# One weight piece converted per tile from tile 1 on, its clamp on GpSimdE, and other assumed VectorE times

## The chip, the cores and the metric

The kernel runs on one core of a Trainium2 chip. The time is device microseconds of one execution; runs of one kernel agree within a fraction of a per cent, and the time of a kernel is the median of its runs. Engines are named as in the profile: PE (TensorE matmul) and PEld (its weight loads), DVE (VectorE), ACT (ScalarE), POOL (GpSimdE), SP (SyncE, which here issues every DMA).

## The reference

A block of local and global attention feeds a layer that takes the maximum of three products. Batch, heads, local tokens, global tokens and head size are 8, 8, 512, 32 and 64.

```python
s_g = scale * q_g @ k_all^T ;  out_g = sm(s_g) @ v_all          # 32 global queries see all 544 keys
s_ll = where(|i - j| <= 32, scale * q_l @ k_l^T, -1e9)          # local queries see a window
s_l = concat([scale * q_l @ k_g^T, s_ll]) ; out_l = sm(s_l) @ concat([v_g, v_l])
x = concat([out_g, out_l]) as (B * 544, 512)
h = max(max(x @ w1, x @ w2), x @ w3) ;  out = h @ w_out         # 512 -> 768 -> 512
```

All inputs of attention are float32. The weights `w1`, `w2`, `w3` and `w_out` arrive as float64 (the kernel sees them as int64), so the kernel has to turn them into float32 itself, with integer operations on the bits.

## The kernel before

**Tiles.** The work of attention is cut into 128 tiles `sl` (8 batches x 4 pairs of heads `p` x 4 blocks of 128 queries). A tile has scores (`scores`, lines 307 or 311, softmax in lines 314 to 322, a store of the probabilities into a banded buffer), transposes of them (`trans`, line 334, four to a tile), transposes of the global rows (`transg`, line 355) and the product with V (`pv`, line 375 or 382). The first tiles (scores up to tile 27, products up to tile 25) multiply in plain float32; the later ones split each operand into a high and a low part of the faster `fp32r` form (`split_q`, `split_k`, `split_v`, and `copy`/`sub` pairs in general). Once in four tiles the global queries of the next pair are handled (`glob`, `glob_soft`), with six small DMAs to `probg`.

**The MoE layer.** From iteration 16 on, iteration `sl` also issues 18 matmuls (`fill` 4 + 4 + 3 + 7) of the layer for the batch before (`moe_group`). A batch has 288 of them, so sixteen iterations issue one batch. For each of the six blocks `f` of 128 hidden columns and each of the three weights there are 12 matmuls from `wh[f]` and `wl[f]` (high and low parts; line 413), combined by maximum (line 421) into `h`; then 72 with `woh` and `wol` (line 432). The last batch and the global tokens follow after tile 127.

**Weight pieces.** `pieces` yields 24 pieces: 18 of 128 x 512 from the first three weights, then 6 from `w_out`. `convert` does a piece in three parts: the load of 512 KB into a staging buffer `wraw` (line 162); then Abs on ACT (line 167), a clamp to a range of exponents on DVE (line 168) and three integer operations on DVE (lines 169 to 171: mask and shift, merge with the sign, merge with the low word); then the split into high (a `copy`) and low part (a `sub`). `weight_step` finishes one piece, starts the second part of the next and issues the load of the one after that, so step number s loads piece s + 1, starts piece s - 1 and finishes piece s - 2. `WS[sl]` says how many steps iteration `sl` makes: 5 in iterations 3 to 11, then mostly 2 in each. The staging buffers share the tags `h0` to `h5` with the hidden blocks of the layer; `STAGE` gives six to the first twelve pieces, then three, then two, and `h5` alone to pieces 21, 22 and 23. The results in float32 lie in `cut` (pieces 0 to 17), which shares its memory with `woh`; `early`, the probabilities of the first 16 tiles, shares its memory with `wol`.

**Sharing out.** `copy`, `sub` and `times` choose their engine when the program is written: `least` takes the engine whose running total `load` plus the assumed cost of this operation is smallest, and `spend` adds the assumed cost of work that has a fixed engine. `settle(4500)` in each iteration keeps an idle engine's total from falling far behind. A scheduler then orders each engine's instructions; each engine works through its own list in order.

Of the kernel before, what the change touches and what calls it, by code (L numbers as in the profile page):

```python
# [10 lines left out]
F32R = mybir.dt.float32r  # L11
# [3 lines left out]
ALU = mybir.AluOpType  # L15
# [4 lines left out]
DM, DF = 512, 768  # L20
# [6 lines left out]
HIMAX = float(np.array(0x47EFFFFF, np.int32).view(np.float32))  # L27
# [20 lines left out]
def f32(ap):  # L48
    return ap.bitcast(F32)


def body(ctx, tc, kin, qin, vin, min_, w1, w2, w3, w4, out):
    nc = tc.nc
    act, dve, pool, pe = nc.scalar, nc.vector, nc.gpsimd, nc.tensor

    const = ctx.enter_context(tc.tile_pool(name="const", bufs=1))
# [19 lines left out]
    def spend(e, ns):  # L76
        load[e] += ns
# [18 lines left out]
    def copy(out, a, psum=False):  # L96
        n = width(out)
        c = {"d": n * (1.04 if psum else 0.52) + (160 if psum else 150), "a": n * 0.833 + (150 if psum else 190)}
        if least(c) == "d":
            dve.tensor_copy(out=out, in_=a)  # L100
        else:
            act.copy(out=out, in_=a)  # L102
# [32 lines left out]
    wo = []  # L135
# [3 lines left out]
    def pieces():  # L139
        n = 0  # L140
        for f in range(12):
            for i in range(3 if f < 6 else 1):
                if f < 6:
                    src = (w1, w2, w3)[i][:, f * 128:(f + 1) * 128].rearrange("(k p) f -> p k f", p=128)
                    yield src, 4, n, wh[f][:, i].rearrange("p k f -> p (k f)"), wl[f][:, i].rearrange("p k f -> p (k f)")
                else:
                    if f == 6:
                        wo.extend(const.tile([128, 6, DM], F32R, name=t, tag=t) for t in ("woh", "wol"))
                    yield w4[(f - 6) * 128:(f - 5) * 128], 1, n, wo[0][:, f - 6], wo[1][:, f - 6]
                n += 1  # L150

    def STAGE(n):
# [5 lines left out]
    def convert(piece):  # L158
        src, k, m, dh, dl = piece
        n, i = 512, STAGE(m)  # L160
        r = moe.tile([128, n], mybir.dt.int64, name="wraw", tag=f"h{i}")
        nc.sync.dma_start(out=r.rearrange("p (k f) -> p k f", k=k) if k > 1 else r, in_=src)
        hi = r.bitcast(I32).rearrange("p (n t) -> p n t", t=2)[:, :, 1]
        lo = r.bitcast(I32).rearrange("p (n t) -> p n t", t=2)[:, :, 0]
        yield
        c = cut[:, m % 6] if m < 18 else moe.tile([128, n], I32, name="wct", tag="o", bufs=2)
        act.activation(out=f32(c), in_=r.bitcast(F32).rearrange("p (n t) -> p n t", t=2)[:, :, 1], func=AF.Abs)
        dve.tensor_scalar(out=f32(c), in0=f32(c), scalar1=2.0 ** -15, scalar2=HIMAX, op0=ALU.max, op1=ALU.min)
        dve.tensor_scalar(out=c, in0=c, scalar1=0x07FFFFFF, scalar2=3, op0=ALU.bitwise_and, op1=ALU.logical_shift_left)
        dve.scalar_tensor_tensor(out=hi, in0=hi, scalar=-0x40000000, in1=c, op0=ALU.bitwise_and, op1=ALU.bitwise_or)  # L170
        dve.scalar_tensor_tensor(out=c, in0=lo, scalar=29, in1=hi, op0=ALU.logical_shift_right, op1=ALU.bitwise_or)
        spend("a", 520)
        spend("d", 1900)
        yield
        copy(dh, f32(c))
        sub(dl, f32(c), f32(dh))
        yield
# [76 lines left out]
    def glob(p, step):  # L254
        if p >= B * NP:
            return
        if step == 0:
            pg[p] = [att.tile([64, KW], F32, name="sg", bufs=1)[:, 0:NG], small.tile([64, 2], F32, name="nmg"), small.tile([64, 2], F32, name="zg")]
        s, nm, z = pg[p]
        c0, n = SEG[step]  # L260
        s0 = 384 * step
        ps = psS.tile([128, 512], F32, name="S")
        if 4 * p in NATK:

            pe.matmul(ps[0:64, 0:n], lhsT=kraw[p][:, KW:KW + 2 * SG], rhs=kraw[p][:, c0:c0 + n], start=True, stop=True)  # L265
            in1 = zero[0:64].to_broadcast([64, n])
        else:
            for j in range(2):
                pe.matmul(ps[:, 0:n], lhsT=qgz.rearrange("p j x -> p (j x)")[:, 128 * j:128 * j + 128],  # L269
                          rhs=kst[p][:, j, c0:c0 + n], start=(j == 0), stop=(j == 1))  # L270
            in1 = s[:, s0:s0 + n]
            copy(in1, ps[64:128, 0:n], True)
        dve.tensor_tensor_reduce(out=s[:, s0:s0 + n], in0=ps[0:64, 0:n], in1=in1, scale=-0.125, scalar=3.0e38,  # L273
                                 op0=ALU.add, op1=ALU.min, accum_out=nm[:, step:step + 1])
        spend("d", n * 1.04 + 75)

    def glob_soft(p):
        if p >= B * NP:
# [13 lines left out]
    def scores(sl):  # L292
        if sl >= NS:
            return
        p, t = divmod(sl, 4)
        c0, n = WIN[t]
# [23 lines left out]
        for j in range(2):  # L320
            times(s[:, j, 0:n], s[:, j, 0:n], z[:, j:j + 1])
        nc.sync.dma_start(out=f32(sc[sl])[:, :, 0:n], in_=s[:, :, 0:n])
        spend("d", 2 * (n * 1.04 + 75) + 150)
        spend("a", 2 * (n * 0.833 + 278))

    def trans(sl):
# [130 lines left out]

    mm = [None]

    WS = [0, 0, 0, 1, 0, 1, 0, 1, 0, 1, 0, 1, 2, 2, 1, 2, 2, 1, 2, 2, 1, 2, 2, 1, 2, 2]  # L460

    def fill(n):
        if mm[0]:
# [34 lines left out]
    for sl in range(NS):  # L498
        p, t = divmod(sl, 4)
        b, n = divmod(p, NP)  # L500
# [83 lines left out]
```

## Time and profile before

| | |
|---|---|
| median of 3 runs | 870.15 us (869.43 to 871.0) |
| the profiled execution | 868.76 us, span 867.0 us |
| DMA | 98.53 MB, mean 114 GB/s |
| DVE busy | 617.3 us in 1885 instructions |
| ACT busy | 492.0 us in 1392 |
| POOL busy | 502.9 us in 669 |

The span is from the first instruction to the last; 1.76 us of the profiled execution lie around it. An engine's busy time is an average over stages with different limits, so the stages are read apart in the sections below. In a row of waits, "A x <- B y" means that engine A stood idle before its work on x until B's work on y was done.

### The profile page before, as it was taken

The page shows a single profiled execution, that of the slowest core. Times are in us where ns is not written, and L with a number is a line of the kernel's source. Part 1 is how long each engine was busy: PE and PEld are TensorE (multiplying, and loading weights), DVE is VectorE, ACT ScalarE, POOL GpSimd, SP SyncE. Part 2 cuts the span into 40 slices and gives each one's busy share as a digit, 9 for nine tenths or more (in the row PEclk, how much of TensorE's full clock was granted, in tenths as well). Part 3 has the DMA queues.
Part 4 walks back from the last instruction along what each step waited for, and adds up shares of the span by engine and source line. Part 5 has one row for each costly group of instructions (what it writes and reads, how often), then busy time and mean ns, then how long its engine had stood idle before and what let it go on. Part 6 is the DMA issues. An engine that isn't in the chain of part 4 may idle for free.

```text
span 867.0 us, 15698 instructions
## 1 busy us (share of the span) xinstructions
PE 817.3 (94%) x4452; PEld 677.3 (78%) x4452; DVE 617.3 (71%) x1885; ACT 492.0 (57%) x1392; POOL 502.9 (58%) x669
## 2 busy tenths in 40 slices
PE   5865988799999999999999999999999999999997
PEld 3643766588888788888887888888888888888897
DVE  4678897887788787887788887877877877521111
ACT  3654655566666566766666666666666666411111
POOL 4544657576667666776767666756677665411211
PEclk8876889899999999999999999999999999999999
DMA  6676755334333533343333433353333422100000
GB/s 202 192 222 197 212 182 158 117 93 144 99 101 104 160 110 105 99 133 114 103 107 104 142 102 98 101 161 104 111 110 122 122 78 74 62 24 1 25 25 25
DMA packets 107238, 98.53 MB, mean 114 GB/s; under 512 B 21008, under 2 KB 97936, under 8 KB 107152
## 3 DMA queue, kind: packets, MB, share of 16 engines
q1 hardware_dynamic: 107152, 97.53, 37.0%
q8 instruction: 36, 0.59, 0.3%
q14 instruction: 50, 0.41, 0.2%
HBM read 56.85 MB, written 8.91 MB: 76 GB/s over the span
## 4 chain that ended last, share of the span: by engine, by line
PE 77%; DVE 10%; DMA 6%; issue 2%; POOL 2%; ACT 1%; SPq 1%; DVEq 0%; POOLq 0%; ACTq 0%
PE pm L413 45%; PE pm L432 13%; PE O L382 6%; PE S L311 5%; PE T L334 3%; DMA wraw<-w_in 1%; DMA wraw<-wo_in 1%; PE S L269 1%; DVE wraw L170 1%; DVE xs L100 1%; PE S L265 1%; PE S L355 1%; PE O L375 1%; DVE s L314 1%; DVE kst L94 1%
## 5 line engine op out<-in xcount | busy, mean ns | idle before, releaser
L413 PE MATMUL pm<-xs,wh 128*128 128x512 f32 (+1 forms) x1296 | 411.2, 390 | 0.0
L413 PEld LDWEIGHTS pm<-xs,wh 128*128 128x128 f32 x1296 | 235.3, 191 | 31.6
L413 PE MATMUL pm<-xs,wl 128*128 128x512 f32 (+1 forms) x648 | 254.9, 393 | 0.0
L112 POOL TENSOR_SCALAR s<-s,z 128x224 f32<-128x224 f32 (+1 forms) x243 | 111.6, 472 | 87.7 <-ACT lox L102 46.7
L316 ACT ACTIVATE s<-s,nm 128x192 f32<-128x192 f32 (+1 forms) x256 | 118.0, 462 | 48.6 <-DVE nm L314 44.0
L413 PEld LDWEIGHTS pm<-xs,wl 128*128 128x128 f32 x648 | 123.6, 191 | 23.5 <-issue 2.4
L432 PE MATMUL pm<-woh,h 128*128 128x512 f32 x408 | 135.2, 400 | 1.3 <-POOL h L94 1.1
L94 POOL TENSOR_TENSOR h<-m,h 128x512 fp32r<-128x512 f32 (+1 forms) x54 | 69.3, 1284 | 99.2 <-ACT h L102 99.2
L94 POOL TENSOR_TENSOR qs<-qraw,qs 128x256 fp32r<-128x256 f32 x100 | 79.5, 795 | 68.6 <-ACT qs L102 42.0
L421 DVE TENSOR_TENSOR m<-pm,m 128x512 f32<-128x512 f32 (+1 forms) x108 | 71.0, 657 | 63.0 <-PE pm L413 62.7
L94 DVE TENSOR_TENSOR pt<-T,pt 128x512 fp32r<-128x512 f32 x102 | 70.4, 691 | 36.2 <-ACT pt L102 33.8
L432 PEld LDWEIGHTS pm<-woh,h 128*128 128x128 f32 x408 | 74.6, 188 | 15.4 <-POOL h L94 4.3
L314 DVE CUSTOM_DVE_ANT_0 s<-S,mask 128x192 f32<-128x192 f32 (+1 forms) x232 | 77.5, 370 | 9.9 <-PE S L307 5.2
L432 PE MATMUL pm<-wol,h 128*128 128x512 f32 x204 | 81.7, 401 | 0.0
L94 POOL TENSOR_TENSOR vs<-vraw,vs 128x256 fp32r<-128x256 f32 x102 | 75.7, 743 | 9.0 <-ACT vs L102 4.2
L102 ACT CAST pt<-T 128x512 fp32r<-128x512 f32 x83 | 48.4, 583 | 47.6 <-PE T L334 47.6
L382 PEld LDWEIGHTS O<-pt,vs 128*128 128x128 f32 x408 | 66.4, 188 | 9.2
L382 PE MATMUL O<-pt,vs 128*128 128x320 f32 (+1 forms) x408 | 72.8, 299 | 0.0
L102 ACT CAST qs<-qraw 128x256 fp32r<-128x256 f32 x85 | 34.6, 407 | 64.3 <-PE S L311 64.0
L334 PEld LDWEIGHTS T<-identr,prob 128*128 128x128 f32 x448 | 51.3, 143 | 24.9 <-issue 5.0
L311 PEld LDWEIGHTS S<-kst,qs 128*128 128x128 f32 x400 | 59.5, 190 | 11.2 <-DVE nmg L273 2.8
L102 ACT CAST h<-m 128x512 fp32r<-128x512 f32 (+1 forms) x54 | 32.3, 597 | 60.5 <-DVE m L421 60.4
(99 smaller groups left out, 1340.5 us busy)
## 6 DMA issues: line engine op xcount, KB each, us to landing
vraw<-v_in SPq DMA_DIRECT2D x128, 128.0 KB, 2.6
qraw<-q_in SPq DMA_DIRECT2D x100, 128.0 KB, 2.2
prob<-s SPq DMA_DIRECT2D x56, 224.0 KB, 2.4
prob<-s SPq DMA_DIRECT2D x56, 192.0 KB, 2.3
wraw<-w_in SPq DMA_DIRECT2D x18, 512.0 KB, 4.5
out_dram<-o SPq DMA_DIRECT2D x32, 256.0 KB, 2.6
kraw<-k_in SPq DMA_DIRECT2D x25, 320.0 KB, 3.1
qn<-q_in SPq DMA_DIRECT2D x28, 128.0 KB, 3.5
```

Of the source, the lines that this page charges most:

```text
L94: (dve if least(c) == "d" else pool).tensor_tensor(out=out, in0=a, in1=b, op=ALU.subtract)
L100: dve.tensor_copy(out=out, in_=a)
L102: act.copy(out=out, in_=a)
L112: pool.tensor_scalar(out=out, in0=a, scalar1=col, scalar2=1.0, op0=ALU.mult, op1=ALU.mult)
L311: pe.matmul(ph[j][:, 0:n], lhsT=qs[sl][:, a, 128 * j:128 * j + 128], rhs=kst[p][:, j, c0:c0 + n], start=(a == 0), stop=(a == 1))
L314: dve.tensor_tensor_reduce(out=s[:, j, 0:n], in0=ph[j][:, 0:n], in1=mask[:, (1, 0, 1, 0)[t], 32 * (t == 0):32 * (t == 0) + n], scale=-0.12 ...
L316: act.activation(out=s[:, j, 0:n], in_=s[:, j, 0:n], func=AF.Exp, bias=nm[:, j:j + 1], scale=-1.0, accum_out=z[:, j:j + 1])
L334: i = pe.transpose(pr[:, 256 * j + 128 * c:256 * j + 128 * c + 128], s[:, j, 128 * c:128 * c + 128], identr)
L382: pe.matmul(o[:, j, 0:320].rearrange("p (a q) -> p a q", a=2)[:, :, 0:n], lhsT=vs[sl][:, 2 * j + c].rearrange("p a d -> p (a d)"), rhs=pt[ ...
L413: pe.matmul(ps[:, 0:n], lhsT=w[f][:, i, k], rhs=xs[k][:, a, 0:n], start=(q == 0), stop=(q == 11))
L421: dve.tensor_tensor(out=m[:, 0:n], in0=ps[:, 0:n], in1=m[:, 0:n], op=ALU.max)
L432: pe.matmul(ps, lhsT=hh[f][:, a, 128 * t:128 * t + 128], rhs=w[:, f], start=(q == 0), stop=(q == 17))
```

## The change

The list `WS` becomes one step in each of the iterations 1 to 25. The clamp of each piece (24 in all) is issued on POOL instead of DVE. `woh` and `wol` are allocated when piece 18 is split instead of when it is loaded, so that `cut` is still there for pieces that are loaded earlier than before. And the assumed costs change: the DVE operations on scores with a running minimum count 220 ns plus the elements instead of 75, the rest of a tile's softmax 440 instead of 150, and a conversion 650 on ACT, 900 on POOL and 2100 on DVE instead of 520 on ACT and 1900 on DVE. These are numbers in the program text: they change which engine `copy`, `sub` and `times` choose.

```diff
                 else:
-                    if f == 6:
-                        wo.extend(const.tile([128, 6, DM], F32R, name=t, tag=t) for t in ("woh", "wol"))
-                    yield w4[(f - 6) * 128:(f - 5) * 128], 1, n, wo[0][:, f - 6], wo[1][:, f - 6]
+                    yield w4[(f - 6) * 128:(f - 5) * 128], 1, n, f - 6, None
...
         act.activation(out=f32(c), in_=r.bitcast(F32).rearrange("p (n t) -> p n t", t=2)[:, :, 1], func=AF.Abs)
-        dve.tensor_scalar(out=f32(c), in0=f32(c), scalar1=2.0 ** -15, scalar2=HIMAX, op0=ALU.max, op1=ALU.min)
+        pool.tensor_scalar(out=f32(c), in0=f32(c), scalar1=2.0 ** -15, scalar2=HIMAX, op0=ALU.max, op1=ALU.min)
...
-        spend("a", 520)
-        spend("d", 1900)
+        spend("a", 650)
+        spend("p", 900)
+        spend("d", 2100)
         yield
+        if m >= 18:
+            if not wo:
+                wo.extend(const.tile([128, 6, DM], F32R, name=t, tag=t) for t in ("woh", "wol"))
+            dh, dl = [w[:, dh] for w in wo]
         copy(dh, f32(c))
...
-        spend("d", n * 1.04 + 75)
+        spend("d", n * 1.04 + 220)
...
-        spend("d", 2 * (n * 1.04 + 75) + 150)
+        spend("d", 2 * (n * 1.04 + 220) + 440)
...
-    WS = [0, 0, 0, 1, 0, 1, 0, 1, 0, 1, 0, 1, 2, 2, 1, 2, 2, 1, 2, 2, 1, 2, 2, 1, 2, 2]
+    WS = [0] + [1] * 25
```

The two spacings, as iteration: steps made before it, are 12: 5 and 11; 16: 12 and 15; 20: 19 and 19; 24: 25 and 23 (before, and with the change). In the whole program ACT gets 94 instructions more (among them the conversion copies of 15 `qs`, 15 `kst`, 14 `qgz`, 13 `vs`, 9 `xs`, 8 `pt` and 6 `wh` that DVE had), DVE 128 fewer, POOL 34 more (24 clamps and 7 subtractions for `kst` among them). PE's instructions are the same ones.

In the order of instructions, first DVE, from the first to the second maximum of the MoE layer (`m` is the running maximum, `cut` and `wraw` belong to weight pieces, ISA rows are the score operations with a running minimum). Before the change:

```order
L421 TENSOR_TENSOR m<-pm,m 128x512
L168 TENSOR_SCALAR cut<-cut 128x512
L318 TENSOR_SCALAR z<-z 128x2
L169 TENSOR_SCALAR cut<-cut 128x512
L319 RECIPROCAL z<-z 128x2
L273 ISA sg,nmg<-S,zero 64x160
L273 ISA nmg 64x1
L170 SCALAR_TENSOR_TENSOR wraw<-wraw,cut 128x512
L168 TENSOR_SCALAR cut<-cut 128x512
L171 SCALAR_TENSOR_TENSOR cut<-wraw 128x512
L169 TENSOR_SCALAR cut<-cut 128x512
L421 TENSOR_TENSOR m<-pm,m 128x512
```

The same stretch with the change, where the conversion's lines are numbered 2 lower than before (the mask, old 169, is 167) and those further down 3 higher (the maximum, old 421, is 424):

```order
L424 TENSOR_TENSOR m<-pm,m 128x512
L276 ISA sg,nmg<-S,zero 64x160
L276 ISA nmg 64x1
L321 TENSOR_SCALAR z<-z 128x2
L284 TENSOR_TENSOR nmg<-nmg 64x1
L322 RECIPROCAL z<-z 128x2
L167 TENSOR_SCALAR cut<-cut 128x512
L286 TENSOR_SCALAR zg<-zg 64x1
L168 SCALAR_TENSOR_TENSOR wraw<-wraw,cut 128x512
L424 TENSOR_TENSOR m<-pm,m 128x512
```

Six rows of conversion stood between the two maxima, and now there are two; the clamp (old line 168) is no longer on DVE.

Second ACT, around the Abs of the pieces of `w_out` (`wct` <- `wraw`), before the change:

```order
L102 CAST woh<-wct 128x512
L167 ACTIVATE wct<-wraw 128x512
L316 ACTIVATE s,z<-s,nm 128x192 x2
L102 COPY xr<-O 128x160
L167 ACTIVATE wct<-wraw 128x512
L102 COPY pt<-S 128x2x32
L102 CAST woh<-wct 128x512
L102 COPY pt<-T 128x4x128
```

and with it, where `pt<-T` is the copy of a tile's transposes, one to a tile:

```order
L165 ACTIVATE wct<-wraw 128x512
L102 COPY pt<-T 128x4x128
L102 CAST qs<-qraw 128x256
L102 CAST woh<-wct 128x512
L319 ACTIVATE s,z<-s,nm 128x192 x2
L102 COPY xr<-O 128x160
L285 ACTIVATE sg,zg<-sg,nmg 64x544
L102 COPY pt<-S 128x2x32
L165 ACTIVATE wct<-wraw 128x512
L102 COPY pt<-T 128x4x128
```

Two Abs stood within one tile, with the exponentials of a tile between them; now there is one to a tile.

Third POOL in the first tiles (`s<-s,z` is the normalisation of a tile's probabilities, two to a tile). Before:

```order
L112 TENSOR_SCALAR s<-s,z 128x192 x2
L94 TENSOR_TENSOR wl_108<-cut,wh_102 128x512
L112 TENSOR_SCALAR s<-s,z 128x192 x2
L112 TENSOR_SCALAR s<-s,z 128x224 x4
L112 TENSOR_SCALAR s<-s,z 128x192 x2
L112 TENSOR_SCALAR sg<-sg,zg 64x544
```

With the change:

```order
L112 TENSOR_SCALAR s<-s,z 128x192 x2
L166 TENSOR_SCALAR cut<-cut 128x512 x2
L112 TENSOR_SCALAR s<-s,z 128x192 x2
L94 TENSOR_TENSOR wl_108<-cut,wh_102 128x512
L112 TENSOR_SCALAR s<-s,z 128x224 x2
L94 TENSOR_TENSOR wl_108<-cut,wh_102 128x512
```

The first two clamps now stand between the normalisations of two neighbouring tiles, and the second subtraction has moved ahead of others.

## The prediction

> **What bounds the kernel now.** I began with the page: shares of each engine, then the slices of the span.
>
> ```profile
> PE 817.3 (94%) x4452; PEld 677.3 (78%) x4452; DVE 617.3 (71%) x1885; ACT 492.0 (57%) x1392; POOL 502.9 (58%) x669
> ...
> PE   5865988799999999999999999999999999999997
> ...
> DVE  4678897887788787887788887877877877521111
> ...
> PEclk8876889899999999999999999999999999999999
> ```
>
> PE is full from about the tenth slice on (a slice is 21.7 us). What is not full lies before 200 us, so the question is what those first nine slices consist of. The tiles can be counted in the transposes (line 334, four to a tile). Tiles 0 to 15 read `early`, later ones `prob`; each iteration issues the transposes of the next tile.
>
> ```profile
> L334 PE MATMUL T<-identr,prob x448: 220/245/341, 79.9 to 753.1; 128*128 128x128 f32 x150
> L334 PE MATMUL T<-identr,early x64: 227/252/562, 20.1 to 73.4; 128*128 128x128 f32 x64
> ...
> 86.43 0.72 PE L334 MATMUL T<-identr,prob 128*128 128x128 f32 x4 [2.89 <-DMA prob<-s]
> ...
> 199.57 0.46 PE L334 MATMUL T<-identr,prob 128*128 128x128 f32 x4
> ```
>
> Tile 0 is at 20.1 us, tile 16 at 79.9, so 86.43 is tile 17 (issued in iteration 16, where the MoE matmuls of batch 0 begin) and, counting on, 199.57 is tile 32. That gives four stages. In the table of windows the columns are the window, its length, busy us of PE, PEld, DVE, ACT and POOL with counts, the granted clock, DMA share and GB/s:
>
> ```profile
> 20.00:86.43 66.43, 44.78 (x276) 32.15 (x277) 48.07 (x166) 37.88 (x118) 32.18 (x44) 0.76 0.67 201
> 86.43:199.57 113.14, 102.56 (x522) 79.22 (x523) 95.61 (x244) 65.11 (x179) 74.93 (x83) 0.92 0.50 154
> 199.57:752.92 553.35, 550.84 (x3035) 464.26 (x3034) 444.00 (x1398) 363.29 (x1038) 369.75 (x508) 1.00 0.37 110
> 752.92:867.00 114.08, 109.35 (x590) 94.84 (x588) 20.41 (x39) 18.13 (x36) 16.33 (x17) 1.00 0.06 21
> ...
> 86.43:167.00 80.57, 70.29 (x357) 52.75 (x358) 69.91 (x162) 44.52 (x119) 51.44 (x52) 0.90 0.56 173
> 102.34:108.58 6.24, 6.24 (x37) 4.90 (x35) 6.24 (x13) 4.24 (x10) 4.23 (x4) 1.00 0.62 171
> ...
> 199.57:222.69 23.12, 23.12 (x129) 19.62 (x128) 18.07 (x60) 16.43 (x45) 14.81 (x23) 1.00 0.44 129
> ```
>
> The third stage is PE throughout (550.84 of 553.35 us), and so nearly is the fourth: little to win or lose. The second stage is the one to look at. Four tiles at full PE take 23.12 us in the later, split form of attention, 5.78 each. In the whole-precision form a tile at full PE takes 6.24 us (102.34 to 108.58, PE busy all the time, and DVE too). From tile 17 to tile 32 are fifteen iterations. Scores run three tiles ahead and are in the first form up to tile 27, so iterations 16 to 24 are of that kind and 25 to 30 of the other: 9 x 6.24 + 6 x 5.78 = 90.8 us. The stage took 113.1: **22.3 us are lost there**. The waits between 86 and 200 us say to whom (who waited for whom: us in total, times, longest):
>
> ```profile
> ACT s L316 <- DVE nm L314: 9.2, 7, 3.1
> ACT wct L167 <- DMA wraw<-wo_in: 8.2, 3, 3.6
> ACT wh L102 <- DVE cut L171: 7.1, 5, 2.7
> ...
> DVE wct L168 <- ACT wct L167: 4.9, 3, 2.6
> ```
>
> All four are the weight conversion or softmax work queued behind it. At the end of it pieces 21, 22 and 23 share one staging buffer (`h5`), so each load starts only when the piece before has been converted. With two steps in one iteration ACT stands at its Abs for 8.2 us in three waits, and DVE behind ACT for 4.9. Ahead of that DVE is simply full: 69.91 of 80.57 us.
>
> **The change, part by part.** First the conversion's own DVE work. These are the windows of the instructions on tile `cut` (first two rows) and `wct` (third), DVE alone, the few casts from `cut` included; the last two rows are line 168, the clamp:
>
> ```profile
> 20.00:86.43 66.43, 27.31 (x39) 0.76 0.67 201
> 86.43:167.00 80.57, 26.94 (x35) 0.90 0.56 173
> ...
> 86.43:167.00 80.57, 16.87 (x24) 0.90 0.56 173
> ...
> 20.00:86.43 66.43, 4.88 (x9) 0.76 0.67 201
> 86.43:167.00 80.57, 12.36 (x14) 0.90 0.56 173
> ```
>
> Early, nine pieces cost 27.31 us, 3.03 each, of it 0.54 for the clamp. Later, fourteen cost 26.94 + 16.87 = 43.8, 3.13 each, the clamp 0.88. Why one clamp costs 0.41 or 3 us is in these rows (min/median/max in ns; then two neighbours in time):
>
> ```profile
> L168 DVE TENSOR_SCALAR cut<-cut x18: 407/426/2996, 16.0 to 123.0; 128x512 f32<-128x512 f32 x18
> ...
> 88.17 1.28 POOL L94 TENSOR_TENSOR wl<-cut,wh 128x512 fp32r<-128x512 f32 x1 [1.59 <-DVE wh L100]
> 88.25 1.49 DVE L168 TENSOR_SCALAR cut<-cut 128x512 f32<-128x512 f32 x1
> ```
>
> The clamp began just after a POOL subtraction and finished 0.29 us after it, instead of after 0.41 us. The Trainium skill, SBUF — State Buffer, section "SBUF: two separate sides", has the rule: VectorE and GpSimd share a port pair as an exclusive lock for a whole instruction, and the loser waits. The trace agrees at this spot. By that rule the moved clamp is not free for DVE, which is the fourth rival below.
>
> *Second stage, the new spacing.* With one step in each iteration from 1 on, pieces 0 to 14 have been begun before iteration 16 (0 to 11 by the old list), so 9 are left instead of the 14 that the trace shows after 86 us. DVE's other work there was 69.91 - 43.8 = 26.1 us, 2.6 for each of ten tiles. Now 9 x (3.13 - 0.88) = 20.3 us join it: 46.4 in ten tiles, 4.6 a tile beside PE's 6.24. DVE no longer fills the tile. MoE uses 1.5 pieces per iteration (18 matmuls, 12 to a piece): with 14 finished at its start and one more per iteration, piece 17 is finished at iteration 19 and read at 27, piece 23 at 25 and read at 28. The `h5` chain remains but gets an iteration (6.2 us) per piece, where a load takes 4.5 (median, row below) and the conversion 2 to 3: it gets about even, so I leave 1 to 2 us of its 8.2. With clock and semaphore losses I keep **4 us** of the 22.3 (bounds 1 and 12), so the stage gives **-18.3 us**.
>
> ```profile
> wraw<-w_in SPq DMA_DIRECT2D x18, 512.0 KB, 4.5
> ...
> L112 POOL TENSOR_SCALAR s<-s,z 128x224 f32<-128x224 f32 x128 | 58.6, 470 | 45.7 <-ACT lox L102 24.8 <-DVE z L319 8.4 <-ACT pt L102 5.5
> ...
> L94 POOL TENSOR_TENSOR wl<-cut,wh 128x512 fp32r<-128x512 f32 x18 | 24.3, 1352 | 19.8 <-ACT wh L102 13.6 <-DVE wh L100 5.7 <-DVE z L318 0.4
> L112 POOL TENSOR_SCALAR sg<-sg,zg 64x544 f32<-64x544 f32 x32 | 23.0, 719 | 40.5 <-ACT pt L102 26.6 <-ACT o L102 7.3 <-DVE zg L284 4.3
> ```
>
> *The clamp on POOL* is not in this trace. The nearest rows are the same kind of instruction with 224 elements (470 ns) and 544 (719): 0.78 ns for each further element, 0.69 us at 512. The ends are 0.47 and the two-input form's 1.35; I take **0.7**.
>
> *First stage.* Five more pieces come into the 66.4 us before tile 17. DVE: 48.07 - 27.31 = 20.8 of other work, less the copies that the new costs send to ACT, plus 14 x 2.49 = 34.9. The copies are (early window, DVE):
>
> ```profile
> L100 DVE COPY pt<-T 128x512 f32<-128x512 f32 x4 | 2.7, 684 | 0.5 <-PE T L334 0.5
> ...
> L100 DVE COPY xr<-O 128x160 f32<-128x160 f32 x4 | 1.3, 323 | 1.1 <-PE O L375 1.0
> ...
> L100 DVE COPY pt<-S 128x64 f32<-128x64 f32 (+1 forms) x4 | 0.9, 236 | 1.3 <-PE S L355 1.3
> ```
>
> So DVE comes to 20.8 - 4.9 + 34.9 = 50.8, against 48.1. POOL gets 14 clamps and 5 subtractions: 32.2 + 9.8 + 6.8 = 48.8. ACT gets 5 Abs, 9 casts and these copies; the rows below give 3.4 + 5.6, and the copies 4.4 by ACT's 0.59, 0.29 and some 0.23 us: 37.9 + 13.4 = 51.3. No engine fills the stage; it is bound by chains (scores, softmax, store, transpose). These get a little longer in three queues, and lose the waits behind an Abs whose load had only just been issued:
>
> ```profile
> L167 ACT ACTIVATE cut<-wraw 128x512 f32<-128x512 f32 x10 | 6.7, 673 | 4.9 <-DMA wraw<-w_in 4.9
> ...
> L102 ACT CAST wh<-cut 128x512 fp32r<-128x512 f32 x5 | 3.1, 619 | 7.4 <-DVE cut L171 7.4
> ...
> POOL s L112 <- ACT cut L167: 6.0, 1, 6.0
> ```
>
> Loads now stand two iterations ahead of their Abs in time, where two steps in one iteration had them next to each other. I take **+2 us**, near DVE's 2.7 more; the ends are -5 (the 4.9 us at Abs gone, nothing else) and +15 (POOL's 16.6 us more, nearly all in the chain).
>
> *Third stage.* The dearer DVE costs move about 90 copies to ACT and seven `kst` subtractions to POOL. PE is busy for 550.84 of 553.35 us with ACT and POOL at two thirds, so they are covered: **0**. Were the cover thin, the wait to grow is PE's for POOL's `h` (6 waits, 3.9 us in this stage). Ends -2 and +5. The fourth stage has no conversion: 0. The allocation of `woh`/`wol` later in the program adds no instruction.
>
> ```profile
> PEld pm L432 <- POOL h L94: 3.9, 6, 1.3
> ```
>
> **Sum.** -18.3 + 2 + 0 = -16.3 us. The profiled execution took 868.76 us (span 867.0 and 1.76 around it): 852.5. The median shown is 870.15, 1.4 above it; I forecast **853**.
>
> **Rivals.**
> 1. *The first stage eats the gain.* The pieces are only carried from where DVE was full to where softmax chains wait for the same three engines. For it: ACT's and POOL's loads rise by a third to a half. Against it: none passes 51 of 66 us. Price: +10 to +15 there instead of +2: 861 to 866.
> 2. *The change does not do what it says.* The loss was the `h5` chain of loads, which stays; loads and conversions of 21 to 23 just stall later. Price: the 8.2 us at Abs remain: 853 + 6 = 859. Against it: nothing needs piece 23 before iteration 28.
> 3. *GpSimd's queue makes it slower.* The clamp now stands in POOL's queue between the normalisations (line 112) whose stores feed the transposes. POOL waits for ACT's Abs, and that for a load; the 6.0 us row shows POOL held by an Abs once already. With 15 clamps before tile 17 this decides from 1.2 us of chain delay for each (18 us eat the gain); at 1.7 us the time is 853 + 15 x 1.7 - 2 = 877. Against it: the loads are early, so an Abs should rarely wait.
> 4. *The port pair.* Each clamp on POOL holds up a VectorE instruction for its 0.7 us: nine in the second stage (DVE 4.6 to 5.2 a tile, still below 6.24) and fourteen in the first (DVE 50.8 to 60.6 of 66, where chains would feel it). Price: of the 9.8 us in the first stage I let 6 through: 859. The page named above gives the rule for it; the casts that leave DVE speak against it.
>
> **How the numbers follow.** Forecast 0.56, rivals 0.16, 0.08, 0.10 and 0.10 in their order. The forecast's own range is 844 to 860 (stage one from -4 to +5, stage two keeping 1 to 8 of the 22.3); rivals 2 and 4 lie in it, and to take in rival 1 the range goes to 866. Beyond it stays rival 3, and below it a first stage that gets much shorter. A difference under 0.2% (1.7 us) cannot be told from none: faster 0.86 (forecast, 2, 4, most of 1), within it 0.04 (1 and 3 at their edges), slower 0.10.
>
> **What would show it.** In the changed profile tile 32's transposes should come at about 183 us instead of 199.6, tile 17's at 88 (83 to 92), with nearly full PE and 6.2 to 6.6 us a tile between them. DVE should be below 80% there, the waits of ACT for `wo_in` below 2 us in all, and the clamp on POOL should take about 0.7 us. From tile 32 to the end it should take 667 us as before. A tile 17 after 100 us, or POOL waiting on Abs for more than 10 us in all, would prove me wrong.

## The result and the profile after

The changed kernel is slower: 894.04 us (median of 4 runs, 893.55 to 894.25) against 869.88 us for the kernel before; the ratio is 1.0275, with a 95% interval of 1.0257 to 1.0293. The forecast was 853.0 with a range of 844 to 866. The profiled execution has a span of 892.5 us, 25.5 more than before.

The page of the changed kernel, engines' shares and four rows of the slices (22.3 us each):

```profile
PE 823.1 (92%) x4452; PEld 680.4 (76%) x4452; DVE 562.7 (63%) x1757; ACT 528.2 (59%) x1486; POOL 546.3 (61%) x703
...
PE   5735496899999999999999999999999999999997
...
DVE  4545546667777777786777777777777677521111
...
POOL 5667666687566766676667766676667664511200
PEclk8756689799999999999999999999999999999999
```

DVE did lose work: 562.7 us busy instead of 617.3. But PE's row has 57354968 ahead of its nines where it had 58659887, and its low digits lie in the first seven slices, before 156 us. The timeline of PE gives tile 17 and tile 32 of the changed kernel:

```profile
113.08 0.34 PE L337 MATMUL T<-identr,prob 128*128 128x128 f32 x1 [5.27 <-DMA prob<-s]
...
226.66 0.37 PE L337 MATMUL T<-identr,prob 128*128 128x128 f32 x3
```

Tile 17 comes at 113.1 us, where it came at 86.4. The four stages, cut at the tiles as in the prediction (window, length, busy us of PE, PEld, DVE, ACT, POOL, then granted clock, DMA share, GB/s):

```profile
20.00:113.08 93.08, 51.51 (x278) 34.55 (x276) 49.91 (x159) 49.95 (x148) 63.46 (x61) 0.65 0.54 166
113.08:226.66 113.58, 102.09 (x521) 79.39 (x521) 72.58 (x197) 64.28 (x181) 82.13 (x87) 0.91 0.43 135
226.66:778.39 551.73, 550.02 (x3034) 464.46 (x3033) 412.36 (x1326) 388.24 (x1099) 373.45 (x520) 1.00 0.36 111
778.39:892.50 114.11, 109.36 (x590) 94.85 (x588) 20.48 (x39) 18.13 (x36) 16.27 (x17) 0.99 0.06 22
```

The first stage is 26.7 us longer, the second 0.4 us longer instead of 18 shorter, the third 1.6 shorter, the fourth the same. In the first stage DVE, ACT and POOL are busy for 54%, 54% and 68% of the time, PE for 55%: no engine is full, and everything waits in turn. The waits between 20 and 113 us say for whom (who waited for whom: us, times, longest):

```profile
ACT wh L102 <- DVE cut L169: 26.3, 10, 5.8
DVE cut L167 <- POOL cut L166: 25.8, 10, 4.9
...
PE O L378 <- ACT pt L102: 18.2, 4, 10.6
...
POOL cut L166 <- ACT cut L165: 3.4, 1, 3.4
```

Read from below: POOL hardly waits for the Abs of a piece, DVE waits 25.8 us for POOL's clamp, ACT 26.3 us for DVE's last merge, and PE 18.2 us for ACT. The instructions of line 166, the clamp on POOL (min/median/max in ns), and who waited for them in the whole program:

```profile
L166 POOL TENSOR_SCALAR cut<-cut x18: 1914/1916/2344, 16.8 to 131.7; 128x512 f32<-128x512 f32 x18
L166 POOL TENSOR_SCALAR wct<-wct x6: 1915/1916/2079, 142.7 to 182.1; 128x512 f32<-128x512 f32 x6
...
  DVE cut L167: 38.4, 14
  DVE wct L167: 14.2, 5
```

One clamp takes 1.92 us, not the 0.7 of the forecast; it took DVE 0.41 where nothing disturbed it. Here is the longest stall that it makes, in the timeline of the changed kernel (start, duration, engine, line, instruction; in brackets the idle time before it and who ended it):

```profile
55.79 0.58 PE L310 MATMUL S<-kn,qn 128*128 128x224 f32 x1
...
56.37 1.21 ACT L165 ACTIVATE cut<-wraw 128x512 f32<-128x512 f32 x2
56.48 1.27 POOL L94 TENSOR_TENSOR xs<-xr,xs 128x512 fp32r<-128x512 f32 x1
...
57.71 1.26 POOL L94 TENSOR_TENSOR wl<-cut,wh 128x512 fp32r<-128x512 f32 x1
...
59.06 3.80 POOL L166 TENSOR_SCALAR cut<-cut 128x512 f32<-128x512 f32 x2
61.01 0.83 DVE L167 TENSOR_SCALAR cut<-cut 128x512 int32<-128x512 int32 x1 [4.91 <-POOL cut L166]
61.92 0.69 DVE L168 SCALAR_TENSOR_TENSOR wraw<-wraw,cut 128x512 int32<-128x512 int32 x1
62.65 0.69 DVE L169 SCALAR_TENSOR_TENSOR cut<-wraw 128x512 int32<-128x512 int32 x1
...
63.37 0.62 ACT L102 CAST wh<-cut 128x512 fp32r<-128x512 f32 x1 [5.79 <-DVE cut L169]
...
64.07 1.51 POOL L94 TENSOR_TENSOR wl<-cut,wh 128x512 fp32r<-128x512 f32 x1 [1.22 <-ACT wh L102]
64.50 1.63 DVE L169 SCALAR_TENSOR_TENSOR cut<-wraw 128x512 int32<-128x512 int32 x1
66.05 0.38 DVE L317 CUSTOM_DVE_ANT_0 s<-S,mask 128x224 f32<-128x224 f32 x1
66.16 0.62 ACT L102 CAST wh<-cut 128x512 fp32r<-128x512 f32 x1 [2.17 <-DVE cut L169]
...
66.69 0.21 ACT L102 COPY pt<-S 128x64 f32<-128x64 f32 x1
...
66.95 1.23 PE L378 MATMUL O<-pt,vraw 128*64 128x160 f32 x8 [10.57 <-ACT pt L102]
```

PE's scores (line 310) are done at 56.4, the Abs of two pieces at 57.6. POOL has two subtractions ahead of the clamps and finishes the first clamp near 61.0. DVE, which takes its instructions in order, stands idle for 4.91 us and then works off both pieces before it reaches the scores at 66.05, 9.7 us after they were there. ACT stands at the casts of the pieces (5.79 and 2.17 us), with the small `pt` copy behind them, and PE stands for 10.57 us.

### The profile page after: what moved, and what is told of

Read it like the earlier page. It is cut to its first block, busy times and chain, and to the rows that moved or that the text cites. A ratio compares the mean times of both kernels' runs of the same rounds, so it can differ in the third digit from the quotient of the medians.

```text
span 892.5 us, 15732 instructions
## 1 busy us (share of the span) xinstructions
PE 823.1 (92%) x4452; PEld 680.4 (76%) x4452; DVE 562.7 (63%) x1757; ACT 528.2 (59%) x1486; POOL 546.3 (61%) x703
## 4 chain that ended last, share of the span: by engine, by line
PE 76%; DVE 2%; POOL 2%; DMA 2%; ACT 2%; issue 1%; POOLq 0%; ACTq 0%; DVEq 0%
PE pm L416 45%; PE pm L435 14%; PE O L385 6%; PE S L314 5%; PE T L337 4%; DMA prob<-s 2%; PE S L272 1%; ACT s L319 1%; POOL kst L94 1%; PE S L358 1%; DVE wraw L168 1%; POOL wct L166 1%; POOL s L112 0%; DVE wct L167 0%; DMA kraw<-k_in 0%
## 5 line engine op out<-in xcount | busy, mean ns | idle before, releaser
L112 POOL TENSOR_SCALAR s<-s,z 128x224 f32<-128x224 f32 (+1 forms) x245 | 107.7, 452 | 82.6 <-ACT lox L102 39.1
L94 POOL TENSOR_TENSOR qs<-qraw,qs 128x256 fp32r<-128x256 f32 x100 | 74.1, 741 | 64.9 <-ACT qs L102 45.0
L321 DVE TENSOR_SCALAR z<-z 128x2 f32<-128x2 f32 x128 | 56.7, 443 | 60.7 <-ACT s L319 60.3
L317 DVE CUSTOM_DVE_ANT_0 s<-S,mask 128x192 f32<-128x192 f32 (+1 forms) x232 | 77.5, 371 | 14.1 <-PE S L310 6.6
L102 ACT CAST pt<-T 128x512 fp32r<-128x512 f32 x91 | 53.2, 585 | 48.1 <-PE T L337 47.1
L94 POOL TENSOR_TENSOR kst<-kraw,kst 64x576 fp32r<-64x576 f32 x50 | 71.8, 1436 | 3.9
L102 ACT CAST qs<-qraw 128x256 fp32r<-128x256 f32 x100 | 40.7, 407 | 56.5 <-PE S L314 53.5
```

The costliest lines, as they stand in the source:

```text
L94: (dve if least(c) == "d" else pool).tensor_tensor(out=out, in0=a, in1=b, op=ALU.subtract)
L112: pool.tensor_scalar(out=out, in0=a, scalar1=col, scalar2=1.0, op0=ALU.mult, op1=ALU.mult)
L317: dve.tensor_tensor_reduce(out=s[:, j, 0:n], in0=ph[j][:, 0:n], in1=mask[:, (1, 0, 1, 0)[t], 32 * (t == 0):32 * (t == 0) + n], scale=-0.12 ...
L321: dve.tensor_scalar(out=z, in0=z, scalar1=1e-9, scalar2=None, op0=ALU.add)
```

## The experiments

Tile 17 and the second stage (tile 17 to tile 32) are counted in each trace as above. Ratios are against runs of the kernel before on the same chip. The two columns on the right come from one execution of each kernel: one that is the same as the kernel before until its last layer (it is described below, with seven forms of one POOL instruction at its end) had tile 17 at 86.0 and a second stage of 114.9, so differences of some 2 us in these columns show nothing.

| kernel | median us | ratio (95%) | tile 17 at | second stage |
|---|---|---|---|---|
| before | 869.88 | | 86.4 | 113.1 |
| changed | 894.04 | 1.0275 (1.0257 to 1.0293) | 113.1 | 113.6 |
| changed, clamp on DVE | 868.40 | 0.9985 (0.9971 to 1.0000) | 99.5 | 101.0 |
| before, clamp on POOL | 896.61 | 1.0314 (1.0293 to 1.0335) | 94.6 | 133.0 |
| before, new spacing | 870.82 | 1.0005 (0.9991 to 1.0019) | 99.7 | 103.1 |
| before, new costs | 862.99 | 0.9924 (0.9904 to 0.9945) | 85.3 | 111.3 |
| changed, clamp replaced by multiplications | 874.51 | 1.0049 (1.0030 to 1.0068) | 101.4 | 105.9 |
| clamp and casts on DVE | 868.33 | 0.9982 (0.9970 to 0.9995) | 94.1 | 105.1 |
| new costs, late single steps | 866.25 | 0.9957 (0.9940 to 0.9973) | 87.8 | 110.7 |
| clamp on DVE, one merge twice | 874.75 | 1.0056 (1.0038 to 1.0074) | 99.1 | 105.3 |
| clamp on DVE, no mask, one merge less | 856.58 | 0.9845 (0.9819 to 0.9871) | 88.2 | 98.0 |
| new costs, conversion counted 3000 | 863.71 | 0.9925 (0.9905 to 0.9945) | 87.5 | 109.6 |
| before, no clamp | 865.63 | 0.9945 (0.9925 to 0.9966) | 86.8 | 107.7 |
| before, five loads twice | 872.67 | 1.0028 (1.0015 to 1.0040) | 89.4 | 113.9 |
| before, five conversions twice | 875.79 | 1.0067 (1.0049 to 1.0085) | 97.5 | 108.2 |

### The parts one by one

The changed kernel with the clamp put back on DVE:

```diff
-        pool.tensor_scalar(out=f32(c), in0=f32(c), scalar1=2.0 ** -15, scalar2=HIMAX, op0=ALU.max, op1=ALU.min)
+        dve.tensor_scalar(out=f32(c), in0=f32(c), scalar1=2.0 ** -15, scalar2=HIMAX, op0=ALU.max, op1=ALU.min)
```

> The changed kernel with the clamp back on DVE, all assumed costs and the spacing as in the change. Theory L (the clamp takes 1.92 us on POOL, and DVE's and ACT's queues stand behind it): the loss goes and what was forecast of spacing and costs comes: tile 17 at 84 to 92 us, 848 to 860 us in all. Theory S (five more pieces before tile 17 stretch the first stage): tile 17 stays after 100 us, 880 us or more. Theory C (ACT, which took over DVE's copies, is the engine that holds the chain up): also 880 or more, with the waits of PE for ACT's copy of the transposes still near 20 us.

The kernel before with only the clamp moved:

```diff
-        dve.tensor_scalar(out=f32(c), in0=f32(c), scalar1=2.0 ** -15, scalar2=HIMAX, op0=ALU.max, op1=ALU.min)
+        pool.tensor_scalar(out=f32(c), in0=f32(c), scalar1=2.0 ** -15, scalar2=HIMAX, op0=ALU.max, op1=ALU.min)
```

> The kernel before with the clamp on POOL and nothing else changed. L: slower than before, by 10 to 30 us (880 to 900), with DVE waiting for POOL's clamp for 30 us or more. S and C: within 5 us of before (865 to 875), since neither spacing nor costs changed.

The kernel before with only the new spacing (and the later allocation of `woh` and `wol`, which it needs):

```diff
-    WS = [0, 0, 0, 1, 0, 1, 0, 1, 0, 1, 0, 1, 2, 2, 1, 2, 2, 1, 2, 2, 1, 2, 2, 1, 2, 2]
+    WS = [0] + [1] * 25
```

> The new spacing alone, clamp on DVE, old costs. L: the spacing is good by itself, 850 to 862 us, tile 17 by 92 us and fewer than 12 us lost between tile 17 and tile 32. S: tile 17 after 100 us, slower than before. C: no opinion beyond the spacing's gain, 850 to 862.

The kernel before with only the new assumed costs:

```diff
-        spend("a", 520)
-        spend("d", 1900)
+        spend("a", 650)
+        spend("p", 900)
+        spend("d", 2100)
...
-        spend("d", n * 1.04 + 75)
+        spend("d", n * 1.04 + 220)
...
-        spend("d", 2 * (n * 1.04 + 75) + 150)
+        spend("d", 2 * (n * 1.04 + 220) + 440)
```

> The new assumed costs alone, old spacing, clamp on DVE. C: slower than before, by 5 us or more. L and S: within 6 us of before on the faster side (864 to 870), since DVE, which is full between 86 and 167 us, loses copies.

The clamp alone costs 26.4 us on top of the kernel before (896.61 against 870.23 on the same chip), and taking it back from the changed kernel saves 25.6. It is the whole slowdown, whatever the spacing. So theory L was right about the clamp, but not about the rest: it expected 848 to 862 us from the spacing with the clamp on DVE, and 868.40 and 870.82 were measured, with tile 17 at 99.5 and 99.7 us instead of by 92. S and C, which expected 880 or more with the clamp back on DVE, were wrong about the time; the longer first stage that S spoke of is there. The spacing alone changes nothing that can be told from none. The costs alone gain 0.76%, and 862.99 us is the best time of all kernels here that leave no operation out; with the spacing beside them 0.15% is left, which can hardly be told from none. Why the two do not add up was not traced further.

### Why the clamp costs 26 us

First its length: the changed kernel with the two operations of the clamp replaced by two multiplications by one, in the same place of POOL's queue:

```diff
-        pool.tensor_scalar(out=f32(c), in0=f32(c), scalar1=2.0 ** -15, scalar2=HIMAX, op0=ALU.max, op1=ALU.min)
+        pool.tensor_scalar(out=f32(c), in0=f32(c), scalar1=1.0, scalar2=1.0, op0=ALU.mult, op1=ALU.mult)
```

> The changed kernel with the clamp's two operations on POOL replaced by two multiplications by 1 (the clamp is left out). If the length of the clamp on POOL is the price: the instruction takes about 0.7 us instead of 1.92 and the time falls to 868 to 876, near that of the clamp on DVE (868.4). If the price is the hop over a third engine's queue: 0.7 us too, but 882 us or more.

The instructions of line 166 in that kernel, and who waited for them:

```profile
L166 POOL TENSOR_SCALAR cut<-cut x18: 607/617/824, 15.7 to 117.8; 128x512 f32<-128x512 f32 x18
L166 POOL TENSOR_SCALAR wct<-wct x6: 611/617/1052, 127.5 to 164.1; 128x512 f32<-128x512 f32 x6
...
  DVE cut L167: 19.4, 11
  DVE wct L167: 12.2, 5
```

The same kind of instruction on the same tile takes 0.62 us with multiplications, close to what I had extrapolated for the clamp, and DVE's waits fall from 52.6 to 31.6 us. Against the kernel before, the time falls from 1.0275 to 1.0049: 2.3%, or 20 us, is the length of the clamp. The other 0.6%, between 1.0049 and the 0.9985 with the clamp on DVE, is what the way over a third engine costs even with a short instruction: 5.6 us. How that divides between the wait in POOL's queue, the handing over, and what the two engines do to each other was not measured.

Then which operation makes it long. At the end of the kernel before, POOL gets 21 more instructions on a tile of its own, seven forms three times each:

```diff
+    t = att.tile([128, 512], F32, name="probe", tag="kst")
+    pool.memset(t, 0.5)
+    for _ in range(3):
+        pool.tensor_scalar(out=t, in0=t, scalar1=1.0, scalar2=1.0, op0=ALU.mult, op1=ALU.mult)
+        pool.tensor_scalar(out=t, in0=t, scalar1=2.0 ** -15, scalar2=HIMAX, op0=ALU.max, op1=ALU.min)
...
+        pool.tensor_scalar(out=t, in0=t, scalar1=2.0 ** -15, scalar2=None, op0=ALU.max)
+        pool.tensor_scalar(out=t[:, 0:256], in0=t[:, 0:256], scalar1=2.0 ** -15, scalar2=HIMAX, op0=ALU.max, op1=ALU.min)
```

> The kernel before with 21 more instructions on POOL behind its last layer, on a tile of its own of 128 x 512: seven forms, three times each. By the elements (0.78 ns each, as the normalisation has): 0.7 us for every form of 512. If maximum and minimum are the dear part: mult with mult 0.7 us, max with min 1.9, and one of them with mult in between, about 1.3; 256 elements about 1.0.

Its instructions by line: the two multiplications, maximum and minimum, a maximum alone, and maximum and minimum on half the elements:

```profile
L535 POOL TENSOR_SCALAR probe<-probe x3: 617/617/617, 723.6 to 748.8; 128x512 f32<-128x512 f32 x3
...
L536 POOL TENSOR_SCALAR probe<-probe x3: 1913/1913/1917, 725.0 to 750.4; 128x512 f32<-128x512 f32 x3
...
L539 POOL TENSOR_SCALAR probe<-probe x3: 1492/1492/1500, 732.5 to 757.1; 128x512 f32<-128x512 f32 x3
...
L540 POOL TENSOR_SCALAR probe<-probe x3: 1065/1066/1066, 734.1 to 758.6; 128x256 f32<-128x256 f32 x3
```

At the same size it is the operation that decides: 512 elements take 0.62 us with multiplications and 1.91 with maximum and minimum. The remaining three forms (a maximum with a multiplication, a multiplication with a minimum, and the bound taken from a column) took 1.92 to 1.99 us, where about 1.3 had been expected of the first two; why one such operation beside a multiplication costs as much as two was not found.

### Why the spacing brings nothing

With the clamp on DVE the windows of the first two stages, and four short ones in the first, are:

```profile
20.00:99.49 79.49, 51.31 (x277) 35.10 (x276) 59.07 (x170) 48.24 (x143) 38.41 (x47) 0.66 0.62 194
99.49:200.48 100.99, 95.48 (x522) 75.12 (x523) 77.33 (x209) 65.54 (x187) 66.88 (x77) 0.98 0.49 152
...
50.00:54.00 4.00, 0.72 (x4) 0.56 (x4) 3.06 (x7) 2.86 (x6) 2.09 (x4) 0.50 0.56 170
...
58.00:62.00 4.00, 0.80 (x7) 0.75 (x9) 2.96 (x6) 1.59 (x6) 2.00 (x2) 0.50 0.80 264
62.00:66.00 4.00, 4.00 (x13) 2.10 (x11) 2.51 (x7) 1.69 (x5) 1.26 (x3) 0.50 0.24 73
66.00:70.00 4.00, 3.31 (x24) 2.51 (x25) 2.05 (x9) 2.52 (x9) 0.68 (x1) 0.84 0.82 247
```

The first stage is 13.1 us longer than before, the second 12.1 shorter. Five pieces more have been converted by tile 17 (14 instead of 9), so a piece costs 2.6 us in the first stage and had cost 2.4 in the second. (This kernel has the new costs too. With the spacing alone the first stage is 13.3 us longer and the second 10.0 shorter, 2.7 and 2.0 us a piece.) About half of each difference is time in which PE works, only more slowly or faster: with the same instructions PE is busy for 51.31 us instead of 44.78 in the first stage at a granted clock of 0.66 instead of 0.76 (busy time times clock is 34 both times), and for 95.48 instead of 102.56 in the second at 0.98 instead of 0.92. The short windows show how a wait can be paid for twice: where PE is busy for 0.72 and 0.80 of 4 us the clock stands at 0.50, PE's next full 4 us still run at 0.50, and only then does it rise. The Trainium skill, TensorE: Matmul & The Clock Gate, section "Part 1: The HAM clock gate (the "warmup" mystery)", gives half the rate after some 3.4 us without work and the full rate after as long a busy stretch. The trace has the same two rates with other lengths: PE works from 61.2 us on and the clock rises only after 67, and between 36 and 37 us it had fallen after PE had stood idle for 2.6 us (32.7 to 35.3). The timeline of this kernel where the first stage loses:

```profile
53.92 1.45 POOL L94 TENSOR_TENSOR wl<-cut,wh 128x512 fp32r<-128x512 f32 x1
...
54.29 1.37 DVE L167 TENSOR_SCALAR cut<-cut 128x512 int32<-128x512 int32 x1
...
60.30 0.39 DVE L317 CUSTOM_DVE_ANT_0 s<-S,mask 128x224 f32<-128x224 f32 x1
60.41 0.62 ACT L102 CAST wh<-cut 128x512 fp32r<-128x512 f32 x1 [2.65 <-DVE cut L169]
...
61.20 1.23 PE L378 MATMUL O<-pt,vraw 128*64 128x160 f32 x8 [4.57 <-ACT pt L102]
```

It is the same place as in the changed kernel, with 4.57 us of PE's wait instead of 10.57: DVE converts two pieces ahead of the scores, ACT stands at the cast of a piece ahead of the copy that PE needs. To take ACT out of this chain, the same kernel (clamp on DVE) with every cast of a piece on DVE:

```diff
-        copy(dh, f32(c))
+        spend("d", 512 * 0.52 + 150)
+        dve.tensor_copy(out=dh, in_=f32(c))
```

> Spacing and costs of the change, clamp on DVE, and every piece's cast to its high part on DVE instead of ACT, so that ACT no longer stands at that cast ahead of the copies for PE. If ACT's queue is what a piece costs in the first stage: tile 17 at 90 to 95 us instead of 99.5, 858 to 865 us. If a piece costs its time on DVE wherever it stands (some 2.5 us each): tile 17 at 98 to 104 us, 866 to 875.

Tile 17 came 5.4 us earlier (94.1), and the second stage took 4.1 us longer; the time did not move (868.33 us, where 858 to 865 were expected with tile 17 that early). The place of the cast shifts the loss as the place of the pieces did. Is it the pieces' loads or the engines' work that costs 13 us? The kernel before, with the loads of pieces 2 to 6 issued a second time, into a tile that nothing reads:

```diff
+    dummy = const.tile([128, 512], mybir.dt.int64, name="dummy")
...
+        if 2 <= m <= 6:
+            nc.sync.dma_start(out=dummy.rearrange("p (k f) -> p k f", k=k), in_=src)
```

> The kernel before with the loads of pieces 2 to 6 issued a second time, into a tile that nothing reads: five more loads of 512 KB before tile 12, no more conversion. If the first stage was stretched by the loads of the five more pieces (SP's issue time and the DMA engines): tile 17 at 94 to 100 us instead of 86.4. If by the work on the engines: tile 17 within 3 us of 86.4, 868 to 874 in all.

And with no more loads, but each conversion instruction of the same pieces made twice:

```diff
+        for _ in range(2 if 2 <= m <= 6 else 1):
             act.activation(out=f32(c), in_=r.bitcast(F32).rearrange("p (n t) -> p n t", t=2)[:, :, 1], func=AF.Abs)
             dve.tensor_scalar(out=f32(c), in0=f32(c), scalar1=2.0 ** -15, scalar2=HIMAX, op0=ALU.max, op1=ALU.min)
             dve.tensor_scalar(out=c, in0=c, scalar1=0x07FFFFFF, scalar2=3, op0=ALU.bitwise_and, op1=ALU.logical_shift_left)
...
+        for _ in range(2 if 2 <= m <= 6 else 1):
+            copy(dh, f32(c))
+            sub(dl, f32(c), f32(dh))
```

> The kernel before with every operation of the conversion of pieces 2 to 6 done twice (Abs on ACT, four operations on DVE, cast and subtraction), with no more loads. If the engines' work stretched the first stage: tile 17 at 95 to 102 us, near the 99.5 of five more pieces, and since nothing is gained later, 878 to 886 in all. If it was the loads: tile 17 within 4 us of 86.4.

Five loads move tile 17 by 3.0 us, the work of five pieces by 11.0; together 14.0, where five whole pieces moved it by 13.1. The window of the first stage with the doubled work:

```profile
20.00:97.50 77.50, 52.49 (x284) 36.49 (x284) 63.27 (x189) 44.16 (x128) 39.70 (x49) 0.72 0.61 187
```

DVE has 15.2 us more work than in the kernel before (63.27 against 48.07), and is still idle for 14 of 77.5 us: the work delays the tiles though the engine is not full. The doubled work's second stage is 4.9 us shorter than before, with nothing taken out of it; so part of what the first stage loses comes back in any case: 875.79 us in all, where 878 to 886 were expected. This was not followed further.

### How much DVE's work is worth

To see what taking work from DVE can bring, three kernels change it alone. With the spacing, the costs and the clamp on DVE, the first merge twice:

```diff
         dve.scalar_tensor_tensor(out=hi, in0=hi, scalar=-0x40000000, in1=c, op0=ALU.bitwise_and, op1=ALU.bitwise_or)
+        dve.scalar_tensor_tensor(out=hi, in0=hi, scalar=-0x40000000, in1=c, op0=ALU.bitwise_and, op1=ALU.bitwise_or)
```

> Spacing and costs of the change, clamp on DVE (868.4 us), and the first merge of each piece done twice on DVE (the second changes nothing): 24 times 0.7 to 0.9 us more work for DVE, 17 to 22 us. Theory P (a us of conversion on DVE costs nearly a us of time in either stage, since DVE's list stands between a tile's scores and its softmax): 882 to 890 us, some 10 of them before tile 17 and 7 between tiles 17 and 32. Theory Q (with one step in an iteration DVE has room in the second stage, as the prediction had it): the second stage grows by less than 3 us, 872 to 879 in all.

The same without the mask and the first merge:

```diff
-        dve.tensor_scalar(out=c, in0=c, scalar1=0x07FFFFFF, scalar2=3, op0=ALU.bitwise_and, op1=ALU.logical_shift_left)
-        dve.scalar_tensor_tensor(out=hi, in0=hi, scalar=-0x40000000, in1=c, op0=ALU.bitwise_and, op1=ALU.bitwise_or)
```

> The same kernel without the mask and the first merge of each piece (both left out of the conversion), 24 times 1.2 to 1.5 us less work for DVE, 29 to 36 us. P: 840 to 850 us, with tile 17 at 85 to 90 instead of 99.5 and at most 10 us saved in the second stage, since PE sets its end. Q: 855 us or more.

The kernel before without the clamp:

```diff
-        dve.tensor_scalar(out=f32(c), in0=f32(c), scalar1=2.0 ** -15, scalar2=HIMAX, op0=ALU.max, op1=ALU.min)
```

> The kernel before without the clamp (left out of the conversion): the most that moving it off DVE could bring. The clamp was busy for 17.7 us on DVE. P: 851 to 860 us. If the losses before tile 32 are waits for loads and not DVE's work: 865 to 870.

One merge more costs 6.3 us (874.75 against 868.40), one merge and one mask less gain 11.8. Taking all 24 clamps away, without putting them anywhere, gains 4.4 us (865.63 against 870.01 on the same chip), for the 17.2 us that 23 of them took on DVE by the prediction's rows. So some 4.4 us is the most that a move of the clamp could have brought to the kernel before, even to an engine where it cost nothing.

Neither theory fits. P expected nearly a microsecond for each microsecond of DVE's work, and all three times lie outside its ranges. Q's ranges hold the first two times, but the second stage grew by 4.3 us with the merge twice, where Q allowed less than 3. By the profiles DVE's busy time changed by +16.1 us (594.0 against 577.9), -34.3 (543.7 against 577.9) and -12.3 (604.9 against 617.3), and the time by +6.3, -11.8 and -4.4: between a third and two fifths of a microsecond for each microsecond of the conversion's work on DVE. DVE's busy time fell by less than the 17.2 us of the clamps, since the mask, now the first of a piece's operations on DVE, took 17.5 us in all instead of 13.6. The 865.63 us lie in the range that was expected if the losses were waits for loads, but five doubled loads moved tile 17 by 3.0 us alone.

### The late pieces and the costs

The prediction put the 8.2 us of waits at the end of the second stage down to two steps in one iteration. The kernel with the new costs, and single steps for the last six pieces:

```diff
-    WS = [0, 0, 0, 1, 0, 1, 0, 1, 0, 1, 0, 1, 2, 2, 1, 2, 2, 1, 2, 2, 1, 2, 2, 1, 2, 2]
+    WS = [0, 0, 0, 1, 0, 1, 0, 1, 0, 1, 0, 1, 2, 2, 1, 2, 2, 1, 2, 2, 1, 1, 1, 1, 1, 1]
```

> The new costs with the old spacing up to iteration 19 and single steps in 20 to 25, clamp on DVE: no two steps in one iteration on the staging buffer that pieces 21 to 23 share. If that chain of loads is a loss of its own: tiles 24 to 27, which took 10.6, 6.5 and 10.2 us with the costs alone, come to 6.3 to 7 each, 854 to 860 us. If only the number of pieces converted in a stage counts: 861 to 865, as with the costs alone (863.0).

It is 3.3 us slower than with the costs alone, outside both ranges. Three of the waits in its second stage:

```profile
DVE wct L168 <- ACT wct L167: 7.4, 4, 3.0
...
ACT woh L102 <- DVE wct L171: 6.2, 4, 2.4
...
ACT wct L167 <- DMA wraw<-wo_in: 4.8, 2, 2.5
```

With the costs alone the same three rows had 6.4, 6.9 and 4.1 us. The three steps from tile 24 to tile 27 took 10.6, 6.5 and 10.5 us, with the costs alone 10.6, 6.5 and 10.2. So single steps do not cure the end. The full spacing does: with the clamp on DVE the same steps took 6.3, 6.5 and 6.6 us. What differs is how many pieces are done by tile 24: 23 there, 21 in these two kernels. That speaks for the backlog and against the pairs of steps. It does not clear the chain of loads: with single steps ACT still stands at its Abs for loads of `wo_in` (4.8 us, the last row). A kernel that changes the backlog alone was not run, so the cause of the late gaps stays open.

Last, whether a still dearer conversion sends more copies away from DVE to advantage:

```diff
-        spend("d", 1900)
+        spend("d", 3000)
```

(with the other new costs)

> Old spacing, clamp on DVE, the new costs with a conversion counted as 3000 ns on DVE instead of 2100, so that still fewer copies go there. If the new costs gain by taking copies off DVE before tile 32: 857 to 862 us. If what was to be had is had: 861 to 865, as with the costs alone.

863.71 us is no different from 862.99.

## Why the prediction was wrong

**The clamp on POOL: a term of the sum that was mis-sized.** The step "I take 0.7", with ends of 0.47 and 1.35, came from the normalisation rows, which multiply. The clamp is the same kind of instruction with maximum and minimum, and it takes 1.92 us. The row for a multiplication carries nothing about these operations, so the upper end was not a bound. With an instruction of about the size I had assumed, 20 us of the slowdown go. Of the 41 us between forecast and result these 20 are the largest part; 5.6 are the place of the clamp, 11 the first stage and 6 the second, as they come out with the clamp on DVE, and the third stage takes 1.6 off.

**Where the clamp stands.** The prediction counted DVE, ACT and POOL by their sums (50.8, 51.3 and 48.8 of 66 us) and gave the first stage +2 us because none is full. It is not fullness that decides there. Each piece now passes ACT, POOL, DVE, ACT and POOL in turn, and each of them has work of the tiles queued behind its part. Even 0.62 us in that place cost 5.6 us. Rival 3 had the queue and the sign (877 us), but not the mechanism: POOL hardly waited for Abs (3.4 us between 20 and 113 us, where more than 10 was named as a sign), and DVE waited for POOL and ACT for DVE. The other sign of being wrong, a tile 17 after 100 us, came true (113.1).

**The first stage: +2 forecast.** With the clamp on DVE it was +13.1, with the change whole +26.7. The 13.1 is rival 1, which I priced at 10 to 15 us and gave a chance of 0.16: the pieces were only carried forward. Doubling bears the price out: 3.0 us for five loads and 11.0 for the work of five pieces, in one execution each.

**The second stage: -18.3 forecast.** With the clamp on DVE it was -12.1; with the clamp on POOL, +0.4. Its late half came as said, though it seems by another cause: from tile 24 to tile 28 it took 25.1 us instead of 34.4. The stage still held 10.2 us above the 90.8 that I had worked out, not 4; 5.5 us of it is idle PE. That "DVE no longer fills the tile" did come true in the changed kernel (72.58 of 113.58 us) and brought nothing: DVE stood idle there, 23.5 us of it waiting for POOL's clamp.

**The `h5` reason.** Single steps did not cure the late gaps, so the two steps in one iteration were not the reason for them. The waits for `wo_in`, which were to fall below 2 us, are 2.6 us in the changed kernel, and 5.8 with the clamp on DVE, where the late gaps are gone; so by themselves they were no measure of the loss.

**Rival 4, the port pair.** The Trainium skill, SBUF — State Buffer, section "SBUF: two separate sides", says that whichever engine starts first holds the shared pair for its whole instruction, and counts a VectorE operation with two inputs in SBUF among those that need it. In the changed kernel's stall the trace differs from it for the clamp: the second clamp runs from 60.96 to 62.86 us (the row's end, and half its 3.80 back), and DVE's merge at 61.92, which has two such inputs, ran inside it in its usual 0.69 us. The mask at 61.01 took 0.83 us beside the same clamp instead of 0.43, but it too ended a microsecond before the clamp. For POOL's subtraction it agrees: the merge at 64.50 beside it took 1.63 us. So this rival cost little in this stall, where DVE lost 4.91 us waiting for the clamp's result; over the whole kernel it was not measured by itself.

**What held.** The third stage (-1.6 us for 0, within -2 to +5) and the fourth (0) were right. The costs gave 0.76% by themselves, which the prediction had not seen as a gain: some 1 us in the first stage and 1.9 in the second, about what one execution differs from the next, and 2.6 in the third.

Had the clamp taken 0.7 us, the time would have been about 874.5, by the kernel with multiplications, still 21 us above the forecast: the two stages were wrong beside the clamp.

## What to carry to other kernels

Before an operation moves to another engine, its price there needs a row of the same operation; a row of the same instruction with other arithmetic can be off by three. Work in the middle of a chain over engines that take their instructions in order can cost much although no engine is full on average, because other work is queued behind each waiting instruction: here 24 clamps of 1.92 us on POOL cost some 26 us. What a move can bring at best is seen by leaving the work out (here 4.4 us). Moving work ahead to a stage whose engines were not full gained nothing here, since that stage was bound by such chains.

## What the runs showed of the hardware

On POOL a 128 x 512 float32 tensor-scalar instruction took 0.62 us with two multiplications, 1.49 with one maximum and 1.91 with maximum and minimum; between 256 and 512 elements the last one rose by 0.85 us, 3.3 ns for each further element. DVE does the same clamp in 0.42 us. DVE's mask takes 0.43 us alone, 0.83 beside a POOL clamp and 1.37 beside a POOL subtraction, while a DVE merge beside a POOL clamp took its normal 0.69. With five more pieces in the first stage PE stood idle there for 6.5 us more (28.2 against 21.7) and took 6.5 us more for the same instructions, at a granted clock of 0.66 instead of 0.76. The two need not be equal: in the changed kernel 19.9 us more of idle time came with 6.7 us more of busy time, at 0.65.
